# Products with the softmax's reciprocal and a clamp of weight words: VectorE or GpSimd

## The chip, the core and the metric

The kernel runs on one core of one Trainium2 chip. The metric is the device time of one execution in microseconds (us), median of the runs shown. Below, PE is TensorE (PEld its weight loads), DVE is VectorE, ACT is ScalarE, POOL is GpSimd, and SP is the engine whose queue issues all the transfers spoken of here. L299 means line 299 of the kernel.

## What is computed

Sliding-window attention with a linear bias, then a dense two-layer block with a squared rectifier, then a mixture of eight experts with a balanced gate. Cut to what the change touches:

```python
scores = scale * q @ k.T + bias                     # 4 batches, 8 heads, 576 tokens, head size 64
scores = np.where(mask, scores, -1e9)               # a window of 128 keys
attn = np.exp(scores - scores.max(-1))
attn = attn / (attn.sum(-1) + 1e-09)                # L296, L297, L299
x = attn @ v                                        # 2304 tokens x 512
h = np.maximum(x @ moe_w_in, 0.0)                   # 512 x 2048, float64 weights
x = (h * h) @ moe_w_out                             # 2048 x 512, float64 weights
...
```

The two weight matrices of the dense block come as float64. The kernel reads each number as two 32-bit words and builds a float32 pair from them.

## The kernel before

The work has two halves. The first, to about 600 us of the span, is attention and the dense block, and a scheduler orders each engine's instructions by its own estimates. The second half is the eight experts, in an order written out by hand (from L720 on, the manual schedule), and holds neither of the changed lines.

**Attention.** A unit is a pair of heads of one batch, either its first 384 tokens or its last 192 (`rest`); there are 32 units, with 80 tiles of up to 128 queries in all. `attention_scores` (L257) makes a tile's scores on PE (L282, name `sc`), adds the bias and takes the minimum on DVE (L285, `s` and `m`), takes the exponential and its sum on ACT (L292, `s` and `z`), and on DVE adds 1e-9 (L296), takes the reciprocal (L297) and multiplies (L299), for each of the two heads by itself. `attention_weights` (L302) turns the result on PE (L322, and L313 for the tail tile, name `pt`) and splits it into two float32r parts: ACT makes the high one, DVE the low one (L113, L114, `p`). `attention_values` multiplies with the values (L336, `xo`). PE does a later tile's scores before it turns an earlier tile (one or two tiles ahead, `plan`, L375).

**Dense block.** The tokens are cut into five chunks, the first of 384, and the hidden size into 16 slices `f`. For each chunk and slice, `gemm1` makes `h` (L118 to L120), ACT and DVE make the squared rectifier (L696, L698), ACT and POOL split it into `gh` and `gl` (L109, L110), and `moe1_tail` accumulates `acc` two slices later. In the first chunk alone, each slice's two weight tiles come from the float64 words: `fetch` (L458) loads 128x1024 words (name `u`, three buffers), `narrow` (L434) turns them into a float32 pair, and the pair is stored for the later chunks (L481). There are 32 calls of `narrow`. Each takes the magnitude on ACT (L440), scales the low words on ACT (L442), clamps the magnitude (L443), shifts (L444), joins (L447) and adds (L451) on DVE, and splits on ACT and DVE (L453, L454). The attention of the first 384 tokens comes ahead of the first chunk's products; the attention of the rest is spread between the products of the chunks.

The two lines of the change:

```python
            nc.vector.tensor_scalar_mul(s[:, j, :nk], s[:, j, :nk], z[:, j : j + 1])
...
        nc.vector.tensor_scalar(mag, mag, F64_SMALL, F64_LARGE, op0=ALU.max, op1=ALU.min)
```

Of the kernel before, what the change touches and what calls it, by code (L numbers as in the profile page):

```python
# [12 lines left out]
ALU = mybir.AluOpType  # L13
# [6 lines left out]
F64_SMALL = 2.0 ** -15  # L20
F64_LARGE = 122879.984375


def raw(ap):

    return ap.bitcast(F32)
# [3 lines left out]
def attention_moe_moe2(  # L30
# [12 lines left out]
    nc = tc.nc  # L43
# [118 lines left out]
    def at_ps(name, t, many=early):  # L162
        pool, tag = many[psn[0] % len(many)] if t["alone"] else (ps_at, "at")
        psn[0] += 1
        return pool.tile([P, 512], F32, name=name, tag=tag)
# [91 lines left out]
    def attention_scores(hp, t, i):  # L257

        tail = i == FULL

        kb0, qb0 = (2, 3) if t["rest"] else (0, 0)
        nk = min(S, (i + 1) * P) - max(0, i - 1) * P
        k0 = (max(0, i - 1) - kb0) * P
        c0 = 2 * P - nk if i == 0 else 0
        heads = 1 if tail else 2

        scs = [at_ps("sc", t) for j in range(heads)]
        s = ap.tile([P, 2, 2 * P], F32, name="s", tag="s", bufs=3)
        m = ap.tile([P, 2], F32, name="m", tag="m", bufs=3)
        z = ap.tile([P, 2], F32, name="z", tag="z", bufs=3)  # L270
        ops = []
        for j in range(heads):
            r = slice(0, P) if tail else slice(j * D, (j + 1) * D)
            if tail:
                qh, ql = [x.rearrange("p j c -> p (j c)") for x in t["qt"]]
            else:
                qh, ql = [t[n][r, (i - qb0) * P : (i - qb0 + 1) * P] for n in ("qh", "ql")]
            kh, kl = [t[n][r, k0 : k0 + nk] for n in ("kh", "kl")]
            ops.append(((qh, kh), (qh, kl), (ql, kh)))
        for x in range(3):  # L280
            for sc, (lhs, rhs) in zip(scs, [o[x] for o in ops]):
                nc.tensor.matmul(sc[:, :nk], lhsT=lhs, rhs=rhs, start=x == 0, stop=x == 2)  # L282
        for j, sc in enumerate(scs):
            bj = tbias[:, hp, :nk] if tail else bias[:, 2 * hp + j, c0 : c0 + nk]
            nc.vector.tensor_tensor_reduce(  # L285
                out=s[:, j, :nk], in0=sc[:, :nk], in1=bj, scale=1.0, scalar=3.0e38,
                op0=ALU.add, op1=ALU.min, accum_out=m[:, j : j + 1],
            )
        if tail:
            nc.gpsimd.memset(s[:, 0, nk:], 0.0)  # L290
        for j in range(heads):
            nc.scalar.activation(  # L292
                s[:, j, :nk], s[:, j, :nk], AF.Exp, bias=m[:, j : j + 1], scale=-1.0,
                accum_out=z[:, j : j + 1],
            )
        nc.vector.tensor_scalar_add(z[:, :heads], z[:, :heads], 1e-9)  # L296
        nc.vector.reciprocal(z[:, :heads], z[:, :heads])  # L297
        for j in range(heads):
            nc.vector.tensor_scalar_mul(s[:, j, :nk], s[:, j, :nk], z[:, j : j + 1])  # L299
        t[i] = s  # L300

    def attention_weights(t, i):  # L302
# [104 lines left out]
    def advance(n):  # L407
        for kind, m, i in steps[done[0] : n]:
            b, hp, rest = units[m]
            if kind == "q":  # L410
                if m == NPAIR:
                    tails_ready()
                attention_qk(m, ts[m])
                ts[m]["p"] = {}
            elif kind == "s":
                attention_scores(hp, ts[m], i)
                if i in (1, FULL):
                    attention_v(m, ts[m])
                    load(m + 2)
            else:  # L420
                attention_weights(ts[m], i)
                attention_values(b, hp, ts[m], i)
        done[0] = max(done[0], n)
# [10 lines left out]
    def narrow(src, hi, lo):  # L434

        low, high = src[:, :, 0], src[:, :, 1]
        t = [cv.tile([P, DM], U32, name=f"cv{i}", tag=f"cv{i}", bufs=2) for i in range(4)]

        mag = t[0].bitcast(F32)
        nc.scalar.activation(mag, high.bitcast(F32), AF.Abs)  # L440

        nc.scalar.activation(t[3], low, AF.Copy, scale=2.0 ** -29)  # L442
        nc.vector.tensor_scalar(mag, mag, F64_SMALL, F64_LARGE, op0=ALU.max, op1=ALU.min)  # L443
        nc.vector.tensor_scalar(  # L444
            t[1], t[0], 3, 0x3FFFFFF8, op0=ALU.logical_shift_left, op1=ALU.bitwise_and
        )
        nc.vector.scalar_tensor_tensor(  # L447
            t[2], high, 0xC0000000, t[1], op0=ALU.bitwise_and, op1=ALU.bitwise_or
        )

        nc.vector.tensor_add(t[1], t[2], t[3])  # L451
        w = t[1].bitcast(F32)
        nc.scalar.activation(hi, w, AF.Copy)  # L453
        nc.vector.tensor_sub(lo, w, raw(hi))  # L454
# [18 lines left out]
    def moe1_load(c, f):  # L473
        out = []
        for j, (nm, dr, nb) in enumerate((("a", d_in[f], 3), ("b", d_out[f], 4))):
            hl = mp.tile([P, 2, DM], F32R, name=nm, tag=nm, bufs=nb)
            if c == 0:
                i = 2 * f + j
                fetch(i + 2)
                narrow(words.pop(i), hl[:, 0], hl[:, 1])  # L480
                nc.sync.dma_start(dr, raw(hl))  # L481
            else:
                nc.sync.dma_start(raw(hl), dr)
            hl = [hl[:, 0], hl[:, 1]]
            out.append([x.rearrange("p (k f) -> p k f", k=NK) if nm == "a" else x for x in hl])
        return out
# [766 lines left out]
```

## Time and profile before

| what | us |
|---|---|
| median of 3 runs (2180.19 to 2181.93) | 2181.15 |
| the profiled execution | 2182.91 |
| its span, from the first instruction to the last | 2181.1 |
| busy: PE, DVE, ACT, POOL | 2101.9, 1513.8, 994.5, 1067.0 |
| PE idle in the span | 79.2 |

A busy time is a sum over the span; an engine that is idle while another sets the pace costs nothing. A stretch's limit shows in what PE, the busiest engine, waits for there. Spans on POOL are rough.

### The profile page before, as it was taken

The numbers are of one execution on the slowest core, as the hardware profiler recorded it, in microseconds if no ns is written. First come the engines' busy times: TensorE is split into PE (matmuls) and PEld (weight loads), VectorE is DVE, ScalarE is ACT, GpSimd is POOL, SyncE is SP. The second block draws the span as 40 slices with busy tenths as digits, with TensorE's granted clock in tenths as the row PEclk, the third lists the DMA queues.
The fourth block names the chain that finished last, engine by engine and source line by source line (L and its number), as shares of the span: only waits on it lengthen the run. The fifth ranks groups of instructions, "written<-read, shape, count | busy, mean of one in ns | idle before, by whom it ended". The sixth has DMA issues, their size and how long they took to land.

```text
span 2181.1 us, 32622 instructions
## 1 busy us (share of the span) xinstructions
PE 2101.9 (96%) x11360; PEld 1918.6 (88%) x11360; DVE 1513.8 (69%) x2667; ACT 994.5 (46%) x2050; POOL 1067.0 (49%) x709
## 2 busy tenths in 40 slices
PE   6889999999999899999999999999999999999998
PEld 4778777777888788888888899999999999999998
DVE  7998445443243888888888666667778567777666
ACT  6776445443334345444444444444444544444443
POOL 2212223123244777887878644445456445554442
PEclk9899999999999999999999999999999999999999
DMA  6676545545474877788788977777787877777773
GB/s 185 212 242 212 155 146 162 153 146 174 159 264 155 316 282 270 265 311 293 286 310 299 341 273 259 259 258 259 259 260 265 270 259 255 253 260 266 260 260 124
DMA packets 281730, 525.49 MB, mean 241 GB/s; under 512 B 85584, under 2 KB 129760, under 8 KB 277472
## 3 DMA queue, kind: packets, MB, share of 16 engines
q1 hardware_dynamic: 281568, 523.42, 71.2%
q8 instruction: 91, 1.49, 0.3%
q14 instruction: 71, 0.58, 0.1%
HBM read 379.60 MB, written 143.73 MB: 240 GB/s over the span
## 4 chain that ended last, share of the span: by engine, by line
PE 66%; DVE 21%; ACT 4%; issue 4%; DMA 3%; POOL 1%; SPq 1%; ACTq 0%; POOLq 0%; DVEq 0%
PE g L118 7%; PE y L119 7%; PE g L120 7%; PE g L119 7%; PE y L120 7%; PE y L118 7%; DVE o L904 4%; DVE rl L933 3%; PE h L118 3%; PE acc L118 3%; PE h L120 3%; PE h L119 3%; PE xo L336 3%; PE acc L120 3%; PE acc L119 2%
## 5 line engine op out<-in xcount | busy, mean ns | idle before, releaser
L1073 POOL TENSOR_TENSOR rb<-R,rb 128x768 fp32r<-128x768 f32 x95 | 212.4, 2237 | 334.4 <-ACT rb L1068 306.2
L1104 DVE TENSOR_TENSOR a<-y,a 128x384 f32<-128x384 f32 x434 | 239.8, 553 | 180.0 <-PE y L120 178.1
L1073 POOL TENSOR_TENSOR rt<-R,rt 128x768 fp32r<-128x768 f32 x125 | 238.7, 1922 | 146.7 <-issue 61.7
L110 POOL TENSOR_TENSOR gl<-r,gh 128x512 fp32r<-128x512 f32 (+1 forms) x80 | 98.9, 1237 | 354.5 <-ACT gh L109 339.7
L1068 ACT ACTIVATE rt<-R 128x768 fp32r<-128x768 f32 x128 | 107.7, 842 | 148.6 <-DVE R L1055 90.1
L110 POOL TENSOR_TENSOR w2a<-r,w2a 128x1024 fp32r<-128x1024 f32 x64 | 162.1, 2549 | 26.5 <-ACT w2a L109 26.4
L118 PE MATMUL g<-xt,w1o 128*128 128x384 f32 x512 | 172.7, 337 | 1.4 <-ACT u L809 0.6
L120 PE MATMUL g<-xt,w1o 128*128 128x384 f32 x512 | 172.2, 336 | 0.0
L118 PE MATMUL y<-rt,w2o 128*128 128x384 f32 x512 | 172.1, 336 | 0.1
L120 PE MATMUL y<-rt,w2o 128*128 128x384 f32 x512 | 172.1, 336 | 0.0
L119 PE MATMUL g<-xt,w1o 128*128 128x384 f32 x512 | 172.0, 336 | 0.0
L119 PE MATMUL y<-rt,w2o 128*128 128x384 f32 x512 | 171.8, 335 | 0.0
L119 PE MATMUL y<-w2a,rh 128*128 128x512 f32 x384 | 150.7, 392 | 2.3 <-POOL w2a L110 2.3
L118 PE MATMUL y<-w2a,rh 128*128 128x512 f32 x384 | 150.7, 393 | 0.0
L120 PE MATMUL y<-w2a,rl 128*128 128x512 f32 x384 | 150.1, 391 | 0.0
L698 DVE SCALAR_TENSOR_TENSOR r<-h,r 128x512 f32<-128x512 f32 (+1 forms) x80 | 50.9, 636 | 133.3 <-ACT r L696 133.3
L1050 DVE TENSOR_TENSOR R<-R,pb 128x768 f32<-128x768 f32 x128 | 137.8, 1077 | 5.2 <-ACT R L1163 3.0
L118 PE MATMUL y<-rb,w2o 128*128 128x384 f32 x384 | 129.9, 338 | 2.8 <-DVE a L1104 2.1
L119 PE MATMUL y<-rb,w2o 128*128 128x384 f32 x384 | 130.2, 339 | 2.4 <-POOL rb L1073 2.4
L120 PE MATMUL y<-rb,w2o 128*128 128x384 f32 x384 | 130.0, 339 | 0.0
L120 PE MATMUL g<-xb,w1o 128*128 128x384 f32 x384 | 129.0, 336 | 0.0
L118 PE MATMUL g<-xb,w1o 128*128 128x384 f32 x384 | 128.9, 336 | 0.0
(231 smaller groups left out, 6234.2 us busy)
## 6 DMA issues: line engine op xcount, KB each, us to landing
w1o<-d_w SPq DMA_DIRECT2D x448, 256.0 KB, 3.1
w2o<-d_w SPq DMA_DIRECT2D x224, 512.0 KB, 4.0
d_w<-w1a SPq DMA_DIRECT2D x32, 1792.0 KB, 12.1
d_w<-w2a SPq DMA_DIRECT2D x32, 1536.0 KB, 8.2
a<-d_in SPq DMA_DIRECT2D x64, 512.0 KB, 3.7
b<-d_out SPq DMA_DIRECT2D x64, 512.0 KB, 3.6
r<-in_moe_w_dram SPq DMA_DIRECT2D x64, 512.0 KB, 4.5
u<-in_moe_w_in_dram SPq DMA_DIRECT2D x16, 512.0 KB, 4.7
```

Of the source, the lines that this page charges most:

```text
L110: (eng or nc.gpsimd).tensor_sub(lo, src, raw(hi))
L118: nc.tensor.matmul(ps, lhsT=lh, rhs=rh, start=first, stop=False, **kw)
L119: nc.tensor.matmul(ps, lhsT=lh, rhs=rl, start=False, stop=False, **kw)
L120: nc.tensor.matmul(ps, lhsT=ll, rhs=rh, start=False, stop=last, **kw)
L336: nc.tensor.matmul(dst, lhsT=l, rhs=r, start=first and n == 0, stop=last and n == 5, skip_group_check=True)
L698: nc.vector.scalar_tensor_tensor(g[:, :n], ph[:, :n], 0.0, r[:, :n], op0=ALU.max, op1=ALU.mult)
L904: nc.vector.scalar_tensor_tensor(acc[0][:, i], y, pe[:, i, e : e + 1], acc[0][:, i], op0=ALU.mult, op1=ALU.add)
L933: nc.vector.scalar_tensor_tensor(rl, src, 0.0, raw(rh), op0=ALU.max, op1=ALU.subtract)
L1050: nc.vector.tensor_mul(r, r, pb[:, None, :].to_broadcast([P, 2, HALF]))
L1068: nc.scalar.activation(x[:, 0], R[m, f, h], AF.Copy)
L1073: eng.tensor_sub(x[:, 1], R[m, f, h], raw(x[:, 0]))
L1104: nc.vector.tensor_add(acc[dst][:, dt], ps[:, :HALF], acc[dst][:, dt])
```

## The change

Two operations go from DVE's queue to POOL's, with the same operands and tiles: the product of a head's exponentials with the reciprocal of their sum, and the clamp of the magnitude words.

```diff
@@ attention_scores
         nc.vector.reciprocal(z[:, :heads], z[:, :heads])
         for j in range(heads):
-            nc.vector.tensor_scalar_mul(s[:, j, :nk], s[:, j, :nk], z[:, j : j + 1])
+            nc.gpsimd.tensor_scalar_mul(s[:, j, :nk], s[:, j, :nk], z[:, j : j + 1])
@@ narrow
-        nc.vector.tensor_scalar(mag, mag, F64_SMALL, F64_LARGE, op0=ALU.max, op1=ALU.min)
+        nc.gpsimd.tensor_scalar(mag, mag, F64_SMALL, F64_LARGE, op0=ALU.max, op1=ALU.min)
```

Since the scheduler orders the first half, other instructions move too.

**POOL, the start of the program** (`bias` is the table of biases, `vsplit` the split values, `cv` a magnitude tile, `s` and `z` as above). Before:

```order
L152 AFFINE_SELECT bias<-bias 128x256 x2
L248 TENSOR_TENSOR vsplit_176<-vraw,vsplit_175 128x3x2x64
L248 TENSOR_TENSOR vsplit_170<-vraw,vsplit_169 128x3x2x64
L248 TENSOR_TENSOR vsplit_176<-vraw,vsplit_175 128x3x2x64
L248 TENSOR_TENSOR vsplit_170<-vraw,vsplit_169 128x2x2x64
```

After:

```order
L152 AFFINE_SELECT bias<-bias 128x256 x2
L443 TENSOR_SCALAR cv_291<-cv_291 128x512
L248 TENSOR_TENSOR vsplit_176<-vraw,vsplit_175 128x3x2x64
L443 TENSOR_SCALAR cv_307<-cv_307 128x512
L443 TENSOR_SCALAR cv_323<-cv_323 128x512
L299 TENSOR_SCALAR s<-s,z 128x128 x2
L443 TENSOR_SCALAR cv_339<-cv_339 128x512
L299 TENSOR_SCALAR s<-s,z 128x128 x2
L443 TENSOR_SCALAR cv_897<-cv_897 128x512
L299 TENSOR_SCALAR s<-s,z 128x256 x2
```

The first tile's two products now stand together behind the third clamp, and the second tile's behind the fourth.

**DVE, the same place** (`z` is the sum or its reciprocal). Before, the first reciprocal, with what follows it; after, the same:

```order
 L444 TENSOR_SCALAR cv_324<-cv_323 128x512
+L297 RECIPROCAL z<-z 128x2
+L296 TENSOR_SCALAR z<-z 128x2
+L447 SCALAR_TENSOR_TENSOR cv_325<-u,cv_324 128x512
 L454 TENSOR_TENSOR b<-cv_308,b 128x512
-L447 SCALAR_TENSOR_TENSOR cv_325<-u,cv_324 128x512
-L443 TENSOR_SCALAR cv_339<-cv_339 128x512
 L451 ISA cv_324<-cv_325,cv_326 128x1024
 L444 TENSOR_SCALAR cv_340<-cv_339 128x512
-L299 TENSOR_SCALAR s<-s,z 128x128
```

The reciprocal now comes behind the third shift (L444), and the product that stood behind the fourth is gone from this queue.

**POOL, the middle of the first chunk** (`gl` is the low part of the squared rectifier). After:

```order
L110 TENSOR_TENSOR gl<-r,gh 128x384
L290 MEMSET s 128x64
L443 TENSOR_SCALAR cv_1416<-cv_1416 128x512
L443 TENSOR_SCALAR cv_1521<-cv_1521 128x512
L299 TENSOR_SCALAR s<-s,z 128x256 x2
L443 TENSOR_SCALAR cv_1537<-cv_1537 128x512
L248 TENSOR_TENSOR vsplit_176<-vraw,vsplit_175 128x2x2x64
```

Before, this queue held only the `gl`, `vsplit` and memset rows here; now two products stand behind two clamps, each of which needs its words loaded.

## Rows read from the trace of the kernel before

**Rows 1.** Stretches: us, busy PE, PEld, DVE, ACT, POOL (count), clock, DMA share, GB/s.

```profile
0.00:20.00 20.00, 8.78 (x39) 6.22 (x39) 12.93 (x40) 13.34 (x34) 9.01 (x26) 1.00 0.72 188
20.00:200.00 180.00, 157.75 (x875) 132.22 (x876) 165.06 (x495) 127.80 (x351) 37.42 (x37) 0.93 0.70 217
200.00:600.00 400.00, 395.85 (x2072) 308.31 (x2070) 175.37 (x596) 173.84 (x492) 97.58 (x102) 1.00 0.52 158
600.00:2181.00 1581.00, 1539.47 (x8377) 1471.89 (x8377) 1160.48 (x1538) 679.51 (x1175) 923.00 (x545) 1.00 0.77 265
```

**Rows 2.** Waits of PE, 20 to 200 us: us in total, times, longest.

```profile
PE pt L322 <- DVE s L299: 10.6, 4, 6.0
PE pt L313 <- DVE m L285: 1.9, 1, 1.9
```

**Rows 3.** Timeline of PE: start, us, instruction, idle time before it and its releaser.

```profile
22.87 0.47 PE L322 MATMUL pt<-ident,s 128*128 128x128 f32 x1 [6.02 <-DVE s L299]
...
26.07 0.48 PE L322 MATMUL pt<-ident,s 128*128 128x128 f32 x1 [1.79 <-DVE s L299]
...
27.69 0.69 PE L322 MATMUL pt<-ident,s 128*128 128x128 f32 x2 [1.14 <-DVE s L299]
```

**Rows 4.** DVE's groups by shape, 0 to 200 us: count | busy us, mean ns.

```profile
L447 DVE SCALAR_TENSOR_TENSOR cv<-u,cv 128x512 uint32<-128x512 uint32 x32 | 24.7, 775 | 0.0
L451 DVE CUSTOM_DVE_ANT_0 cv<-cv,cv 128x1024 uint16<-128x1024 uint16 x32 | 22.3, 696 | 0.0
...
L443 DVE TENSOR_SCALAR cv<-cv 128x512 f32<-128x512 f32 x32 | 17.3, 552 | 0.5 <-ACT cv L440 0.4
...
L444 DVE TENSOR_SCALAR cv<-cv 128x512 uint32<-128x512 uint32 x32 | 14.6, 463 | 0.0
L299 DVE TENSOR_SCALAR s<-s,z 128x256 f32<-128x256 f32 x38 | 14.1, 412 | 0.0
L454 DVE TENSOR_TENSOR b<-cv,b 128x512 fp32r<-128x512 f32 x16 | 11.8, 736 | 1.9 <-ACT b L453 1.9
L454 DVE TENSOR_TENSOR a<-cv,a 128x512 fp32r<-128x512 f32 x16 | 11.1, 693 | 1.6 <-ACT a L453 1.6
...
L299 DVE TENSOR_SCALAR s<-s,z 128x128 f32<-128x128 f32 x16 | 4.1, 294 | 0.0
...
L299 DVE TENSOR_SCALAR s<-s,z 128x192 f32<-128x192 f32 x4 | 1.3, 314 | 0.0
```

**Rows 5.** POOL's groups by shape, 0 to 200 us: the one-input instructions.

```profile
L148 POOL TENSOR_SCALAR_AFFINE_SELECT bias<-bias 128x256 f32<-128x256 f32 x8 | 3.0, 399 | 0.0
...
masks.py:199 POOL TENSOR_SCALAR_AFFINE_SELECT ident<-ident 128x128 f32<-128x128 f32 x1 | 0.3, 292 | 0.0
```

**Rows 6.** POOL's groups by shape, 200 to 600 us: two-input instructions.

```profile
L110 POOL TENSOR_TENSOR gl<-r,gh 128x512 fp32r<-128x512 f32 x48 | 61.8, 1287 | 230.7 <-ACT gh L109 215.9 <-PE acc L120 11.4 <-DMA b<-d_out 3.4
...
L248 POOL TENSOR_TENSOR vsplit<-vraw,vsplit 128x256 fp32r<-128x256 f32 x11 | 8.0, 729 | 21.9 <-ACT vsplit L247 21.7
```

**Rows 7.** Single lines on DVE: minimum, median and maximum ns, first and last start.

```profile
L443 DVE TENSOR_SCALAR cv<-cv x32: 406/415/1310, 12.6 to 186.7; 128x512 f32<-128x512 f32 x32
L444 DVE TENSOR_SCALAR cv<-cv x32: 403/416/1071, 14.0 to 189.4; 128x512 uint32<-128x512 uint32 x32
L447 DVE SCALAR_TENSOR_TENSOR cv<-u,cv x32: 675/680/1507, 15.2 to 191.4; 128x512 uint32<-128x512 uint32 x32
```

**Rows 8.** Timeline of POOL: two instructions of the same line.

```profile
76.69 1.01 POOL L110 TENSOR_TENSOR gl<-r,gh 128x384 fp32r<-128x384 f32 x1 [6.54 <-ACT gh L109]
...
85.82 3.68 POOL L110 TENSOR_TENSOR gl<-r,gh 128x384 fp32r<-128x384 f32 x1 [8.03 <-ACT gh L109]
```

**Rows 9.** The chain that ended last, 0 to 210 us: start, us, what.

```profile
41.04 4.45 DMA u<-in_moe_w_in_dram
```

**Rows 10.** Waits of ACT, 20 to 200 us: us in total, times, longest.

```profile
ACT cv L440 <- DMA u<-in_moe_w_in_dram: 4.3, 4, 1.9
```

## The prediction

> **What bounds the kernel now.** I read the stretches first. From 600 us on PE is busy for 1539.47 of 1581 us and nothing that the change names runs; from 200 to 600 us PE is busy for 395.85 of 400 us while DVE has 175.37 and POOL 97.58 [rows 1]. There DVE is no bound, and relieving it can give at most the 4.15 us that PE idles. The stretch that can change is the first: from 20 to 200 us DVE is busy for 165.06 of 180 us (92%), PE for 157.75, ACT for 127.80 and POOL for 37.42 [rows 1]. PE idles 22.25 us there. The list of PE's waits in this stretch says for whom: 10.6 us for the products of L299 themselves, in four waits, then a row of single waits of 1 to 2 us for other DVE results, of which the first is 1.9 us [rows 2]. (A wait that began before 20 us is counted whole in that list.) Since DVE is 92% busy, these are waits for DVE's queue rather than for one instruction. The timeline shows the worst place: PE waits 6.02, 1.79 and 1.14 us for the first two tiles' products [rows 3].
>
> **The change, part by part.**
>
> *What leaves DVE.* Up to 200 us all 32 clamps (17.3 us) and 58 of the 144 products (14.1, 4.1 and 1.3 us), 36.8 us in all [rows 4]. DVE's 12.93 + 165.06 = 178.0 us up to 200 us become 141.2.
>
> *What POOL gets.* The trace has no such instruction on POOL. The near bound is its one-input instruction of the same shape: 399 ns for 256 columns, 292 for 128 [rows 5]; the difference, 107 ns for 128 columns, gives 345 ns for 192 and 613 for 512 as estimates. The far bound is its two-input instruction: 729 ns for 256 columns and 1287 for 512 [rows 6], hence 450 and 590 for 128 and 192. Near: 38 x 0.399 + 16 x 0.292 + 4 x 0.345 + 32 x 0.613 = 40.9 us. Far: 38 x 0.729 + 16 x 0.450 + 4 x 0.590 + 32 x 1.287 = 78.5 us. I take the near one, because both moved operations read one tile from SBUF and write one; the far end stays for the range. The Trainium skill (GPSIMD Engine Reference, section "Engine selection") says the same of one-input work, that it runs at about line rate, against half of VectorE's speed with two inputs; no run here shows it for this instruction.
>
> *What the two engines take from each other.* A clamp on DVE takes 415 ns in the median, but 1310 once, and L444 and L447 have such maxima too, 1071 and 1507 [rows 7]; a `gl` on POOL that takes 1.01 us elsewhere took 3.68 at 85.82 us [rows 8]. So they hold each other up. The means over the medians price it on DVE: (552 - 415) x 32 = 4.4 us, (463 - 416) x 32 = 1.5 and (775 - 680) x 32 = 3.0 [rows 4, 7], 8.9 us beside 9.01 + 37.42 = 46.4 us of POOL, or 0.19 us per us. For 40.9 us more on POOL that is 7.8 us. DVE's load to 200 us is then 141.2 + 7.8 = 149 us of 200 instead of 178: about 76% of the stretch from 20 us on instead of 92%.
>
> *The start (to 28 us).* The first tile's products now follow the reciprocal on an idle POOL, both heads at once, where PE got the two heads at 22.87 and 26.07 us and the second tile at 27.69 [rows 3]. That lets the first tiles go some 3 us earlier. But the words for the fifth tile of weights are on the chain, a 4.45 us load issued at 41.04 us [rows 9], behind a long row of attention loads on SP's queue, which waits for the store of the fourth tile; that store depends on DVE's L454 and moves by less. SP's queue is otherwise only reordered. I take -2 us.
>
> *The rest of the stretch.* Of the 22.25 us, (22.87 - 20) + 1.79 + 1.14 = 5.8 lie at the start; 16.4 remain, nearly all for DVE. The bounds are 0 and -16.4. With DVE's load down by a sixth, its queue still comes late where ACT makes it late (ACT is 71% busy, and waits for loads of words 4.3 us [rows 10]). I take a little under half: -7 us.
>
> *The handover.* A pair of products takes 2 x 0.4 us on POOL, where DVE's pair has 2 x 0.412 [rows 4, 5], but crosses engines, and may stand behind a clamp whose words have not come, or behind a `gl` of 1.29 us [rows 6]. The bounds are nothing, where PE has other tiles to do, and one `gl` for each of the four products that PE waited for today, 5 us. I take +1.
>
> *From 200 us on.* The other 86 products leave a DVE with room and join a POOL that is a quarter busy [rows 1]. The list of PE's waits there names no product, and PE has several us of other work between a tile's scores and its turning. I cost it at nothing. If that cover went, each late tile would cost PE up to one `gl`, 1.29 us; I allow +4.
>
> The sum is -2 - 7 + 1 = -8 us, against the profiled execution's 2182.91 us: 2174.9. That execution is 1.76 us above the median of the runs, so the forecast on their scale is **2173 us**.
>
> **The rivals.**
>
> *POOL's instructions are dearer, and the shared way to SBUF becomes the bound: slower.* The lines that were seen held up read or write SBUF on both engines. If only one of the two engines can do such work at a time, before the change that way is taken to 200 us by DVE's L443, L444, L447, L451, L454 and L299, 36.8 + 14.6 + 24.7 + 22.3 + 22.9 = 121.3 us [rows 4], and POOL's 46.4: 167.7 of 200. After it, DVE has 84.5 left, POOL 46.4 + 40.9: 171.8, still under 200. At the far price it is 84.5 + 46.4 + 78.5 = 209.4, over 200 by 9.4 us: 2190.5 us or more. The point from which it decides is 69 us of new work, 1.7 times the near price, or some 0.68 us for a 256-column product. The Trainium skill has this rule (SBUF — State Buffer, section "Who interferes with whom"): the shared port pair is an exclusive lock, held for a whole instruction, and the later comer blocks. The trace agrees with a blocked `gl` of 3.68 us. Against this rival speaks the 399 ns row.
>
> *Nothing gained: the next wait takes the place.* PE would wait for POOL's products, held behind clamps, or for the words that ACT waits for, as it now waits for DVE. For it speak rows 9 and 10, and that a held-up POOL instruction took 3.68 us. The terms cancel: 2177 to 2185 us. The Trainium skill (Perfetto Trace Analysis, section "Optimizing Scalar/DVE Operations") warns that moving work between these two engines might not help, for the shared port.
>
> *All of it gained.* PE's idle 16.4 us and 3 us at the start go: 2181.15 - 19.4 = 2162 us. PE's granted clock in the stretch, 0.93 between the levels of 2.4 and 1.2 GHz [rows 1], could rise with a busier PE and give some 2 us more; I count none of it in the sum.
>
> **How the numbers follow.** The forecast has a chance of 0.52, nothing gained 0.22, the shared way 0.16, all gained 0.10. A measurement of this kernel can tell about 0.2%, 4.4 us, from no change: faster means below 2176.8, slower above 2185.5. The forecast and the full gain count as faster, 0.62; the second rival as the same, 0.22; the first as slower, 0.16. For a range that holds the time 8 times in 10, I cut half of the full gain's and half of the first rival's: 2160 to 2189 us.
>
> **What would show it.** In the changed profile: POOL's L299 at 0.35 to 0.5 us for 256 columns and L443 near 0.6; DVE's share from 20 to 200 us down to about three quarters; the first turning of a tile at 21 to 22 us with both heads together; PE's waits for DVE in the stretch about halved, and PE's idle time from 200 us on unchanged. I am wrong if POOL's products take 0.7 us or more, if L444, L447 or L451 lengthen in the mean by over 0.25 us each, or if PE's list of waits now names POOL's L299 for 10 us or more.

## The result and the profile after

The change made the kernel **slower**: 2208.99 us (median of 5 runs, 2206.22 to 2220.29) against 2181.61 us for the kernel before in the same rounds (5 runs, 2180.19 to 2183.19). The ratio is 1.0133, 95% interval [1.0118, 1.0147]. The prediction said 2173 us, with a range to 2189. Repeated later, in other rounds, the changed kernel gave 1.0112 [1.0087, 1.0138].

The profiled execution of the changed kernel is the slowest of its five (2220.29 us, span 2218.1). Its stretches, with columns as in [rows 1], the second ending where PE begins the second chunk (its first product `h` with 512 columns, which began at 199.75 us before):

```profile
0.00:20.00 20.00, 8.42 (x39) 6.15 (x39) 10.31 (x33) 10.30 (x26) 12.60 (x28) 1.00 0.60 158
20.00:237.47 217.47, 182.55 (x884) 151.26 (x885) 150.83 (x417) 134.14 (x361) 151.22 (x127) 0.88 0.60 188
237.47:600.00 362.53, 360.19 (x1874) 279.50 (x1874) 140.80 (x475) 161.60 (x460) 155.92 (x174) 0.99 0.51 154
```

All of the loss lies in the first chunk: it ends 37.7 us later, and the span is 37.0 us longer. DVE is now busy for 150.83 of 217.47 us, 69%, where it was 92% [rows 1], but the stretch is longer: up to the second chunk DVE was busy 161.1 us, only 16.6 less than the 177.7 before. PE idles 34.9 us there, and the clock column reads 0.88, where it read 0.93; how far this column can be read is said at e15 below. What happened to the moved instructions shows in the views of single lines (minimum, median, maximum ns):

```profile
L299 POOL TENSOR_SCALAR s<-s,z x144: 596/923/2417, 23.1 to 629.8; 128x256 f32<-128x256 f32 x96, 128x128 f32<-128x128 f32 x32, 128x192 f32<-128x192 f32 x16
...
L443 POOL TENSOR_SCALAR cv<-cv x32: 1908/1921/2355, 13.6 to 214.4; 128x512 f32<-128x512 f32 x32
```

A product, mostly of 256 columns, takes 0.92 us on POOL in the median, against a mean of 0.41 on DVE [rows 4]; a clamp takes 1.92 us against 0.42 [rows 7]. The list of waits, 0 to 260 us (us in total, times, longest), shows who waits:

```profile
DVE cv L444 <- POOL cv L443: 27.2, 14, 3.6
POOL s L299 <- DVE z L297: 23.8, 15, 6.1
PEld pt L322 <- POOL s L299: 23.0, 12, 9.5
...
PE pt L322 <- POOL s L299: 13.7, 8, 9.2
```

DVE stands 27.2 us in front of the shift L444 for POOL's clamp, a wait that didn't exist, and everything else in DVE's queue stands behind it. PE waits 13.7 us for POOL's products, where it waited 10.6 us for DVE's [rows 2]. DVE's groups up to 237 us, with columns as in [rows 4], show the second price:

```profile
L447 DVE SCALAR_TENSOR_TENSOR cv<-u,cv 128x512 uint32<-128x512 uint32 x32 | 26.1, 818 | 0.4
L451 DVE CUSTOM_DVE_ANT_0 cv<-cv,cv 128x1024 uint16<-128x1024 uint16 x32 | 24.4, 764 | 0.3
L444 DVE TENSOR_SCALAR cv<-cv 128x512 uint32<-128x512 uint32 x32 | 19.2, 602 | 27.2 <-POOL cv L443 27.2
```

The same 32 instructions are longer in the mean than before: 818 against 775, 764 against 696, 602 against 463 ns [rows 4]. The start of the program shows both prices together. POOL's timeline (start, us, instruction, idle time before it and its releaser):

```profile
20.22 2.28 POOL L443 TENSOR_SCALAR cv<-cv 128x512 f32<-128x512 f32 x1 [1.84 <-ACT cv L440]
23.14 2.33 POOL L299 TENSOR_SCALAR s<-s,z 128x128 f32<-128x128 f32 x2 [0.63 <-DVE z L296]
25.44 1.92 POOL L443 TENSOR_SCALAR cv<-cv 128x512 f32<-128x512 f32 x1
27.99 1.90 POOL L299 TENSOR_SCALAR s<-s,z 128x128 f32<-128x128 f32 x2 [0.63 <-DVE z L297]
```

And PE's:

```profile
24.75 0.47 PE L322 MATMUL pt<-ident,s 128*128 128x128 f32 x1 [9.24 <-POOL s L299]
...
33.45 0.69 PE L322 MATMUL pt<-ident,s 128*128 128x128 f32 x2 [1.18 <-POOL s L299]
```

The first tile turns at 24.75 us instead of 22.87 [rows 3], and tiles and clamps alternate on POOL at some 2 us each.

### The profile page after: what moved, and what is told of

The parts are those of the page before. It is cut to its first block, busy times and chain, and to the rows that moved or that the text cites. A ratio compares the mean times of both kernels' runs of the same rounds, so it can differ in the third digit from the quotient of the medians.

```text
span 2218.1 us, 32804 instructions
## 1 busy us (share of the span) xinstructions
PE 2129.7 (96%) x11360; PEld 1941.8 (88%) x11360; DVE 1468.0 (66%) x2491; ACT 997.7 (45%) x2050; POOL 1255.5 (57%) x885
## 3 DMA queue, kind: packets, MB, share of 16 engines
q8 instruction: 91, 1.49, 0.3%
## 4 chain that ended last, share of the span: by engine, by line
PE 68%; DVE 18%; ACT 4%; POOL 3%; issue 3%; DMA 2%; SPq 0%; ACTq 0%; POOLq 0%; DVEq 0%
PE y L119 7%; PE y L120 7%; PE y L118 7%; PE g L118 7%; PE g L120 7%; PE g L119 7%; DVE o L904 4%; PE xo L336 3%; DVE rl L933 3%; PE h L118 3%; PE acc L118 3%; PE acc L120 3%; PE h L119 3%; PE h L120 3%; PE acc L119 3%
## 5 line engine op out<-in xcount | busy, mean ns | idle before, releaser
L299 POOL TENSOR_SCALAR s<-s,z 128x256 f32<-128x256 f32 (+1 forms) x144 | 131.6, 924 | 103.3 <-DVE z L297 82.8
L110 POOL TENSOR_TENSOR w2a<-r,w2a 128x1024 fp32r<-128x1024 f32 x64 | 161.1, 2533 | 27.9 <-ACT w2a L109 27.9
L118 PE MATMUL y<-rb,w2o 128*128 128x384 f32 x384 | 129.8, 338 | 2.8 <-DVE a L1104 2.1
L119 PE MATMUL y<-rb,w2o 128*128 128x384 f32 x384 | 130.0, 338 | 2.3 <-POOL rb L1073 2.3
L118 PE MATMUL acc<-gh,b 128*128 128x512 f32 (+1 forms) x320 | 131.3, 410 | 0.0
L118 PE MATMUL h<-xh,a 128*128 128x512 f32 (+1 forms) x320 | 128.3, 401 | 2.3 <-DVE r L698 2.2
```

Source lines behind the costliest of these rows:

```text
L110: (eng or nc.gpsimd).tensor_sub(lo, src, raw(hi))
L118: nc.tensor.matmul(ps, lhsT=lh, rhs=rh, start=first, stop=False, **kw)
L119: nc.tensor.matmul(ps, lhsT=lh, rhs=rl, start=False, stop=False, **kw)
L299: nc.gpsimd.tensor_scalar_mul(s[:, j, :nk], s[:, j, :nk], z[:, j : j + 1])
```

## The experiments

The theories, as the expectations name them. **A**: POOL's price and turn-taking; the loss is time in which DVE and PE wait for POOL's long instructions. **B**: the two engines hold each other up at SBUF, so that POOL's work costs DVE time even if nobody waits for its results. **C**: the scheduler's new order alone. A fourth, **D**, came with the profile: PE's pauses lower the clock that it is granted. All kernels below are the kernel before with the edit shown. "Us" is the ratio's distance from 1 times 2182 us.

| run | on POOL | ratio to before [95%] | us |
|---|---|---|---|
| e1_products | the products | 1.0029 [1.0011, 1.0046] | +6.3 |
| e2_clamp | the clamps | 1.0057 [1.0038, 1.0075] | +12.4 |
| e15_both_again | both (the change) | 1.0112 [1.0087, 1.0138] | +24.4 |
| e12_shadow_products | extra products, nobody waits | 1.0038 [1.0023, 1.0054] | +8.3 |
| e8_shadow_free | extra clamps, nobody waits | 1.0058 [1.0042, 1.0074] | +12.7 |
| e14_shadow_both | both extra loads, nobody waits | 1.0049 [1.0029, 1.0069] | +10.7 |
| e3_shadow | extra clamps that hold a buffer | 1.0109 [1.0067, 1.0150] | +23.8 |
| e7_one_op | the clamps, one operation | 1.0018 [1.0005, 1.0030] | +3.9 |
| e13_both_one_op | both, clamps with one operation | 1.0088 [1.0063, 1.0112] | +19.2 |
| e5_two_input | the products as two-input ones | 1.0040 [1.0021, 1.0058] | +8.7 |
| e4_low | the split's low part (L454) | 1.0071 [1.0052, 1.0089] | +15.5 |
| e6_late | the later tiles' products | 0.9998 [0.9982, 1.0013] | -0.4 |
| e9_swap | nothing | 0.9997 [0.9985, 1.0008] | -0.7 |
| e10_drop_add | nothing; L296 left out | 0.9996 [0.9978, 1.0014] | -0.9 |
| e11_act_one | nothing; half the products on ACT | 0.9992 [0.9977, 1.0007] | -1.7 |

**One part at a time.**

```diff
e1_products
-            nc.vector.tensor_scalar_mul(s[:, j, :nk], s[:, j, :nk], z[:, j : j + 1])
+            nc.gpsimd.tensor_scalar_mul(s[:, j, :nk], s[:, j, :nk], z[:, j : j + 1])
e2_clamp
-        nc.vector.tensor_scalar(mag, mag, F64_SMALL, F64_LARGE, op0=ALU.max, op1=ALU.min)
+        nc.gpsimd.tensor_scalar(mag, mag, F64_SMALL, F64_LARGE, op0=ALU.max, op1=ALU.min)
```

> The 144 products on GpSimd, the clamps back on VectorE. Theory A (price and turn-taking): a GpSimd product takes 0.9 us for 256 columns where VectorE took 0.35, and TensorE waits for the turning behind it; the products cost about half of the loss, +10 to +15 us over the kernel before, and GpSimd's products keep their 0.9 us. Theory B (the two engines block each other at SBUF): the loss goes with GpSimd's added busy time up to the end of the first chunk, some 50 of 113 us, so about +12 us, and VectorE's L444, L447 and L451 lengthen in the mean by over 0.1 us each. Theory C (the scheduler's new order alone): under +5 us, with GpSimd's products not named in TensorE's waits.

> The 32 clamps on GpSimd, the products back on VectorE. Theory A: 1.92 us for a clamp, and VectorE's L444 waits for it 15 to 27 us in all; since VectorE is relieved of 17 us and each weight tile is wanted two slices later, the loss is +5 to +15 us. Theory B: about 63 of 113 us of added GpSimd time, so about +15 us, with L444, L447 and L451 longer by over 0.1 us each. Theory C: under +5 us.

Each part loses by itself, the clamps some twice as much, and the products less than either theory A or B gave for them. The waits of DVE for the clamps alone are far smaller than with both (e2's profiled execution is the fastest of its six):

```profile
DVE cv L444 <- POOL cv L443: 8.6, 6, 3.0
```

8.6 us here, 27.2 with the products on the same queue: there a clamp that is ready stands behind products and a product behind clamps.

**POOL busy, nobody waiting.** e8 and e12 leave DVE all of its work and give POOL a second load of the same shapes, which reads other tiles and writes a scratch tile that nobody reads; e14 has both. In e12 and e14 the reciprocals get eight buffers, so that POOL holds none up; no run has these buffers without the load. (e3 was the first try: its copy reads the magnitude itself and so keeps its buffer from ACT, which then waited 15.3 us for POOL. It mixes A and B.)

```diff
e8_shadow_free, behind L454
+        beside = cv.tile([P, DM], F32, name="beside", tag="beside", bufs=1)
+        nc.gpsimd.tensor_scalar(beside, raw(hi), F64_SMALL, F64_LARGE, op0=ALU.max, op1=ALU.min)
e12_shadow_products, behind L299 (bj: the tile's bias)
+            beside = ap.tile([P, 2 * P], F32, name="beside", tag="beside", bufs=1)
...
+            nc.gpsimd.tensor_scalar_mul(beside[:, :nk], bj, z[:, j : j + 1])
e3_shadow, behind L443
+        nc.gpsimd.tensor_scalar(beside, mag, F64_SMALL, F64_LARGE, op0=ALU.max, op1=ALU.min)
```

> The kernel before, and in addition each clamp is done once more on GpSimd into a tile that nobody reads. VectorE is not relieved and nobody waits for GpSimd's copy, but GpSimd is busy for 61 us more up to the end of the first chunk. Theory A: within +4 us of the kernel before (what the two engines take from each other is small). Theory B: at least as dear as the clamps moved alone, +15 us or more. Theory C: whatever the order gives, within 5 us either way.

> The kernel before, and in addition 32 clamps of 128x512 on GpSimd that read the high part of each weight tile, which is not given free before a product two slices later, and write a tile nobody reads. GpSimd is busy for some 61 us more in the first chunk, and nobody waits for these instructions' results or buffers. Theory A (waiting for GpSimd's results and buffers): within 4 us of the kernel before. Theory B (blocking at SBUF): +8 us or more, and VectorE busy for 10 us more up to the end of the first chunk.

> The kernel before with an extra GpSimd product of the same shapes beside each of DVE's 144 products: it reads the bias tile and the reciprocal and writes a scratch tile that nobody reads (the reciprocals get more buffers, so that nothing waits for it). GpSimd gets the load of the products of L299, some 40 x 1.1 us more up to 200 us, DVE keeps its own, nobody waits for GpSimd. The run with the products alone on GpSimd was 6.4 us slower, with DVE relieved of 19.5 us. Theory A (price and turn-taking: the loss is waiting for the products): 0 to +3 us. Theory B (the engines hold each other up at SBUF): at 0.19 us of DVE per us of GpSimd some 8 us more on DVE, and a loss of 6 to 12 us, as the extra clamps that nobody waits for cost 12 us. Theory C (the scheduler's order alone): any sign, within 5 us.

> The kernel before with both extra loads on GpSimd at once, the 32 clamps that read the weights' high words and the 144 products that read the bias, into scratch tiles: GpSimd gets the changed kernel's work, DVE keeps all of its own, and nothing waits for GpSimd. Alone they cost 12 and 8 us. Theory B (hindrance at SBUF is all of the loss): some 20 to 27 us, and more where the two overlap; the changed kernel, whose DVE is relieved of 37 us, would then lose less than this one. Theory A (the waits for GpSimd are the loss): under 10 us. If B and A share it: 15 to 20 us here, against 27 with the waits.

POOL's work costs time even if nobody waits for it: 12.7 and 8.3 us alone, 10.7 with both, so B is shown to be a part of it, though e14's 10.7 is less than the 15 to 20 expected if A and B share the loss. That the two together cost no more than one I can't explain; the intervals allow some of it ([6.3, 15.1] against a sum of 21 with some 5 either way). The stretches of e14 up to its second chunk:

```profile
0.00:20.00 20.00, 8.78 (x39) 6.22 (x39) 12.71 (x38) 13.01 (x33) 11.23 (x27) 1.00 0.72 190
20.00:211.19 191.19, 165.03 (x873) 138.58 (x874) 180.81 (x498) 128.60 (x351) 163.64 (x125) 0.91 0.66 204
```

DVE is busy 12.71 + 180.81 = 193.5 us with the work that took it 177.7 up to 199.75 us before: 15.8 us more, for 128.7 us more on POOL (174.9 against 46.2), or 0.12 us per us. In e8 it is 11.7 us for 73.6 (0.16), in e12 8.0 for 62.0 (0.13). e14's groups on DVE in the same stretch (the shifted lines are L443, L444, L447, L451, L454 of before):

```profile
L454 DVE CUSTOM_DVE_ANT_0 cv<-cv,cv 128x1024 uint16<-128x1024 uint16 x32 | 24.2, 756 | 0.0
L450 DVE SCALAR_TENSOR_TENSOR cv<-u,cv 128x512 uint32<-128x512 uint32 x32 | 23.2, 731 | 0.0
...
L299 DVE TENSOR_SCALAR s<-s,z 128x256 f32<-128x256 f32 x38 | 17.7, 505 | 0.0
L447 DVE TENSOR_SCALAR cv<-cv 128x512 uint32<-128x512 uint32 x32 | 17.4, 550 | 0.0
L446 DVE TENSOR_SCALAR cv<-cv 128x512 f32<-128x512 f32 x32 | 17.2, 553 | 0.8 <-ACT cv L443 0.8
...
L457 DVE TENSOR_TENSOR b<-cv,b 128x512 fp32r<-128x512 f32 x16 | 14.2, 889 | 1.7 <-ACT b L456 1.7
L457 DVE TENSOR_TENSOR a<-cv,a 128x512 fp32r<-128x512 f32 x16 | 12.0, 749 | 0.1
```

These groups sum to 125.9 us, and POOL's 174.9 make 300.8 us in 211.2. At least 89.6 us of these recorded spans lie side by side. A span can hold time in which the instruction is held up, as the 3.68 us of [rows 8] may, so each form is also counted at its shortest duration in this stretch: DVE's groups then take 102 us and POOL's 147, together 249 us in 211.2. One at a time doesn't hold them, by some 38 us. Hence the engines hinder each other, but the way is not given to one of them alone.

**How long POOL's instruction is.**

```diff
e7_one_op
-        nc.vector.tensor_scalar(mag, mag, F64_SMALL, F64_LARGE, op0=ALU.max, op1=ALU.min)
+        nc.gpsimd.tensor_scalar_max(mag, mag, F64_SMALL)
e13_both_one_op: e7_one_op with e1_products
e5_two_input
-            nc.vector.tensor_scalar_mul(s[:, j, :nk], s[:, j, :nk], z[:, j : j + 1])
+            nc.gpsimd.tensor_mul(s[:, j, :nk], s[:, j, :nk], z[:, j : j + 1].to_broadcast([P, nk]))
```

> The clamp alone on GpSimd, with one of its two operations (the maximum; the minimum is left out). With both it took 1.92 us for 512 columns, and the kernel 12.5 us more. If each operation costs a pass of its own, it takes 1.0 to 1.3 us, DVE's waits for it go from 8.6 to about 4 us, and the loss falls to 5 to 8 us (theories A and B alike, A by the waits, B by GpSimd's 22 us less). If a pass has one price whatever it computes, 1.9 us and +12 us.

> Both moved as in the change, but GpSimd's clamp with one operation (the minimum is left out), 1.49 us instead of 1.92, so that GpSimd has 14 us less to do up to the end of the first chunk. The clamp alone cost 12.5 us with two operations and 3.9 with one, the products alone 6.4. If GpSimd's length of work is what counts (A by the waits, B by the time held), the loss falls from 27 us to 10 to 14. If it stays above 20 us, the length of the clamp is not the cause of what the two cost together.

> The changed kernel once more, on the same chip and in the same rounds as the two others, for comparison with them and for its granted clock over more executions: it was 0.981 to 0.989 in five, against 0.986 to 0.993 in the kernel before. Expected: +25 to +29 us. If pauses of PE lower the granted clock (D), the mean clock stays some 0.003 below that of before, worth 6 to 8 us of the 27, while the runs with one part alone showed the clock of before within 0.001.

> Products on GpSimd as in the run with the products alone, but written as a product of two tiles (the reciprocal repeated along the row), the form in which GpSimd took 0.73 us for 256 columns of the values' split. Clamps on VectorE. Theory A (GpSimd's price): if a product takes 0.73 to 0.8 us instead of 0.92 to 1.15, the time falls below that of the run with the products alone, to +1 to +5 us over the kernel before. Theory B (blocking at SBUF): a second input read from SBUF holds VectorE up more, as the low parts did when they went to GpSimd; +8 us or more, with VectorE's L444 and L451 longer by over 0.15 us in the mean than in the kernel before.

The clamp's line in e7:

```profile
L443 POOL TENSOR_SCALAR cv<-cv x32: 1479/1492/2449, 13.9 to 184.4; 128x512 f32<-128x512 f32 x32
```

The second operation costs 0.43 us of the 1.92, between the two guesses. With 14 us less on POOL the clamp alone loses 3.9 us instead of 12.4, less than the 5 to 8 expected, though with both parts the loss falls only from 24.4 to 19.2, short of what was expected. In e13 DVE still waits for the clamps 19.7 us and PE for products 13.7. In e5 the line of the products reads:

```profile
L299 POOL TENSOR_TENSOR s<-s,z x144: 394/614/1147, 20.2 to 600.5; 128x256 f32<-128x256 f32 x96, 128x128 f32<-128x128 f32 x32, 128x192 f32<-128x192 f32 x16
```

The same product, asked for as a two-input instruction, takes 614 instead of 923 ns in the median. It gained nothing (+8.7 against +6.3, intervals overlapping), but it is no clean test of the length: up to the second chunk POOL was busy 81.9 us in e5 and 107.5 in e1, but DVE 170.7 and 165.2, so part of what POOL saved was paid on DVE.

e15 is the more typical execution of the changed kernel. Its stretches:

```profile
0.00:20.00 20.00, 8.41 (x39) 6.14 (x39) 10.14 (x33) 10.25 (x26) 12.60 (x28) 1.00 0.59 154
20.00:232.09 212.09, 174.47 (x885) 143.79 (x885) 150.12 (x417) 134.33 (x361) 150.66 (x127) 0.93 0.62 193
```

The first chunk ends 32.3 us later than before, and the span is 27.1 us longer. PE idles 91.3 us of the span, 12.0 more than before, and its busy time grows by 15.1 us for the same 11360 matmuls. That is no added work, and it bears on D. The clock column reads 0.93 in the first chunk, as before, and its mean over the five executions is 0.988, over the 13 of before in those rounds 0.989. But the column counts time without a clock record as full clock, and the records begin only at 74.5 us in e15 and at 33.2 us in the kernel before. Which of the two levels (1.2 and 2.4 GHz) PE had until then shows in the multiplications with the values (L336). The first line is the kernel before from 46.9 to 57.0 us, with 0.50 recorded; the second the same from 33.2 to 46.8 us, with 1.00 recorded; the third e15 from 20 to 74.4 us, without a record:

```profile
L336 PE MATMUL xo<-p,vsplit 128*128 128x256 f32 x7 | 2.2, 460 | 0.0
L336 PE MATMUL xo<-p,vsplit 128*128 128x256 f32 x21 | 4.3, 316 | 0.2
L336 PE MATMUL xo<-p,vsplit 128*128 128x256 f32 x42 | 12.7, 456 | 1.1 <-DVE p L114 0.6 <-DMA qraw<-in_q_dram 0.5
```

So in e15 PE ran at the lower level up to 74.5 us, where in the kernel before it rose at 33.2. In the first chunk 289 of e15's 924 matmuls began at the lower level, against 139 of 912. Over the chunk the means of this form nearly agree at each level (456 and 455 ns at the lower, 309 and 298 at the higher), and so do those of the other frequent forms. So the 15.1 us are, as nearly as the trace tells, the clock's, and D is not refuted: more than half of the 27.1 us is PE at its lower level. What that is worth by itself is open. The first record comes at 64 to 75 us in the changed kernel, e1, e5, e7, e13 and e15, and at 33 to 40 us in the kernel before and the other ten; yet e7 loses 3.9 us, and in e5 PE's busy time grows by 14.7 us while its idle time falls by 9.5. Before its rise PE was busy, in the kernel before, for 6.9 of the 13.1 us from 20 us on; in e15 for 5.4 of 16 us from 20 us on and for 34.8 of the next 38.4. Why it stayed low that long, no run here tells.

**What relief of DVE is worth, and other controls.** e6 moves only products behind the first chunk, e11 gives half of them to ACT, e10 leaves out the addition of 1e-9, e9 exchanges two lines of text, and e4 gives POOL another step of `narrow` in the place of the clamp.

```diff
e6_late
-            nc.vector.tensor_scalar_mul(s[:, j, :nk], s[:, j, :nk], z[:, j : j + 1])
+            eng = nc.vector if t["early"] else nc.gpsimd
+            eng.tensor_scalar_mul(s[:, j, :nk], s[:, j, :nk], z[:, j : j + 1])
e11_act_one, for j = 1 alone
+                nc.scalar.activation(s[:, j, :nk], s[:, j, :nk], AF.Copy, scale=z[:, j : j + 1])
e10_drop_add
-        nc.vector.tensor_scalar_add(z[:, :heads], z[:, :heads], 1e-9)
e9_swap
-        nc.scalar.activation(t[3], low, AF.Copy, scale=2.0 ** -29)
         nc.vector.tensor_scalar(mag, mag, F64_SMALL, F64_LARGE, op0=ALU.max, op1=ALU.min)
+        nc.scalar.activation(t[3], low, AF.Copy, scale=2.0 ** -29)
e4_low
-        nc.vector.tensor_sub(lo, w, raw(hi))
+        nc.gpsimd.tensor_sub(lo, w, raw(hi))
```

> Only the products of the later units go to GpSimd (batch 1's last rows and batches 2 and 3, some 84 products, which come after the first chunk); clamps and the earlier products stay on VectorE. TensorE is the bound there. Both theories: within 3 us of the kernel before. If these late products cost over 5 us, the loss is not confined to the first chunk.

> The second head's product of each tile goes from DVE to ACT as a scaled copy, GpSimd gets nothing. DVE loses half of the products, some 10 us up to 200 us; ACT, 71% busy there, gets 29 of them at 0.4 to 0.6 us, some 14 us. Theory A and the prediction's reasoning (a relieved DVE lets PE wait less): -3 to -6 us, if ACT has the room. Theory B: the same sign, since ACT doesn't share GpSimd's way to SBUF: -3 to -6 us. If ACT's queue then comes later than DVE's did (it waits for loads of words, and the product stands behind them): 0 to +8 us, with PE's waits naming ACT's L299.

> The kernel before without L296, which adds 1e-9 to the softmax's sum; a sum that holds exp(0) = 1 does not change by it in float32. It takes 28 small instructions of 0.17 us off VectorE up to 200 us, and off each tile's chain. If VectorE's queue bounds the first chunk, as the prediction had it, 2 to 6 us faster than the kernel before; if not, within 2 us.

> The kernel before with two independent lines of the program's text exchanged, ACT's scaled copy (L442) and DVE's clamp (L443): the same instructions on the same engines, only the scheduler's priorities of the two differ. Theories A and B: no difference, within 3 us. Theory C (the new order of the scheduled program alone makes such differences): some 5 us or more in either direction.

> Clamps and products on VectorE; instead the low part of each weight tile (L454, 32 subtractions with two inputs of 128x512) goes to GpSimd, 1.29 us each there against 0.69 on VectorE. Nobody waits for it before a store and a product two slices later. Theory A: VectorE is relieved of 22 us and no chain gets longer: 3 to 8 us faster than the kernel before. Theory B: GpSimd's 41 us more block VectorE: no gain or up to 8 us slower.

The late products cost nothing, and the exchanged lines move the time by -0.7 us [-3.3, +1.7]: and e6, e10 and e11, which move instructions too, also lie within 2 us of the kernel before. Nothing here shows that a new order alone could cost 24 us, so C is unlikely as the cause. e11 is the answer to the question that the prediction didn't ask. On ACT it has the group

```profile
L300 ACT ACTIVATE s<-s,z 128x256 f32<-128x256 f32 (+1 forms) x28 | 13.2, 471 | 0.1
```

with DVE's first chunk 5.8 us lighter (172.0 busy), and it gains 1.7 us [-5.0, +1.5], which is not told from nothing. PE's longest wait for a product is 5.4 us, in front of the half that stayed on DVE, against 6.0 before [rows 2]:

```profile
PE pt L325 <- DVE s L302: 9.3, 3, 5.4
```

e4 missed by the sign. It took 22.9 us from DVE [rows 4], and DVE was busy 182.0 us up to its second chunk, more than before:

```profile
0.00:20.00 20.00, 8.78 (x39) 6.21 (x39) 12.66 (x35) 12.26 (x31) 10.44 (x27) 1.00 0.68 184
20.00:210.50 190.50, 160.34 (x882) 136.19 (x882) 169.39 (x475) 131.31 (x353) 75.92 (x68) 0.92 0.68 211
```

For 40.2 us more on POOL, what is left on DVE grew by 27.2 us, 0.68 us per us, four to five times the price of the one-input loads that nobody waits for.

**What follows.** Of the 24.4 us, 10.7 [6.3, 15.1] come with POOL's work alone (e14). The other 14, within some 7, come only where its results are needed; this is a difference of two runs, and since no run has the waits without the load, that waiting is the cause of it is argued, not shown. On PE, e15's longer span is 15.1 us of matmuls at the lower clock and 12.0 of idle time; e14's is 8.0 and 3.9. How much of the clock's part follows from PE's waits is open. The wait that grows most when the parts are put together is DVE's for the clamp (8.6 alone; 25.4 in e15). No kernel tried beats the kernel before by more than the measurement can tell.

## Why the prediction was wrong

**The step that failed first: *What POOL gets*.** It took the near price, "because both moved operations read one tile from SBUF and write one": 0.399 us for 256 columns and 0.613 for 512, 40.9 us in all [rows 5]. The first chunk of e15 has these groups:

```profile
L443 POOL TENSOR_SCALAR cv<-cv 128x512 f32<-128x512 f32 x32 | 63.7, 1994 | 10.7 <-ACT cv L440 10.7
L299 POOL TENSOR_SCALAR s<-s,z 128x256 f32<-128x256 f32 x40 | 42.9, 1083 | 16.4 <-DVE z L297 10.8 <-ACT b L453 3.7 <-ACT s L292 1.1
...
L299 POOL TENSOR_SCALAR s<-s,z 128x128 f32<-128x128 f32 x16 | 14.4, 908 | 13.0 <-DVE m L285 5.7 <-DVE z L297 3.9 <-ACT b L453 2.7
```

That is 121.0 us, and 124.6 with the tiles of 192 columns: three times the near price and 1.6 times the far end of 78.5. (The two sums, worked out again, come to 40.8 and 78.4, which changes nothing.) The far end was no bound, since one row of another operation (of two inputs) doesn't bound a form that the trace doesn't hold. The Trainium skill (GPSIMD Engine Reference, section "Engine selection") puts one-input work on GpSimd at about line rate; these rows don't agree, for the one-input product took 923 ns in the median on POOL, where the two-input one took 614 and DVE's 412 in the mean of 256 columns [rows 4].

***What the two engines take from each other*** was right in its price, 0.19 us of DVE per us of POOL: e15's DVE is busy 160.3 us up to its second chunk. Without the moved work (17.3 us of clamps and some 20 of products) 140 were left; 20 us more for 117 on POOL is 0.17. Only the number of us was wrong, 20 instead of 7.8. DVE's share fell to 69 or 71%, below the 76% forecast, but over a longer stretch: its 160.3 us are less than the 177.7 before and more than the forecast 149.

***The handover*** was the second step that failed. It gave +1 us and at most 5, for the products that PE waits for. It left the clamp's own handover out, which the next instruction on DVE needs at once: 25.4 us of waiting on DVE in front of L444 in e15, with all of DVE's queue behind. Its sentence "a pair of products takes 2 x 0.4 us on POOL" is the first step's mistake carried on: the first pair took 2.33 us.

***The start* and *the rest of the stretch*** forecast -2 and -7 us from a relieved DVE. The first tile came 1.9 us later instead of 3 earlier. The reading under it, that a queue busy to 92% makes PE's waits, is not borne out: e11 relieved DVE without touching POOL and gained 1.7 us [-5.0, +1.5], e10 0.9 [-4.8, +3.1]. So the 16.4 us of PE's idle time were no measure of what a lighter DVE gives. e11's relief is small, though, and a larger one without POOL was not tried.

***The clock*** stood at nothing in the sum ("I count none of it in the sum"), and only as a gain. It was a third step that failed: e15's matmuls took 15.1 us more, of which the lower level is, as nearly as the trace tells, the whole. The 1.00 and 0.93 of [rows 1] also hide that the kernel before ran at the lower level up to 33.2 us.

***From 200 us on*** was right: e6 has the products there on POOL and no difference.

**The rivals.** The first ended on the right side, and its deciding point was passed: 124.6 us of new work against 69, 0.92 us for a product against 0.68. Its mechanism holds only in part. With one engine at a time, e14 would have had 102 + 147 = 249 us of work for the shared way even at the shortest durations, which the chunk's 211 us can't hold. The Trainium skill's rule of an exclusive lock (SBUF — State Buffer, section "Who interferes with whom") therefore does not set the time of this mix as a whole, though the lengthened lines and e4 agree that there is a hindrance. Of the prediction's three signs of error two came: products over 0.7 us, and PE waiting over 10 us for POOL's L299. The third, lines longer by over 0.25 us, did not: the largest was 0.14, L444. The second rival, that the next wait takes the place, came in kind (DVE's wait for the clamp) but not in its size, which ended at 2185 us.

## What to carry to other kernels

Price an instruction on GpSimd by a row of the same operation with the same kind of operands, or leave the bound open above: here the form, not the count of inputs, set 0.40, 0.61 or 0.92 us for a tile of mostly 256 columns. When work leaves a busy engine for a slower one, list who needs each result next, and what is queued behind that reader; a chain DVE to GpSimd to DVE stops DVE's whole queue. Before counting on relief, ask what one us less on the busy engine has been shown to buy; here it bought next to nothing. Before reading a clock column, see from where on it has records, and compare matmuls of one form in both kernels.

## What the runs showed of the hardware

GpSimd's product with a scalar per partition (mostly of 256 columns) takes 923 ns in the median, and the same product with the reciprocal broadcast as a second input 614. A clamp of 512 columns takes 1.92 us with two operations and 1.49 with one. What work on GpSimd takes from VectorE beside it depends on the instruction: 0.12 to 0.16 us per us for one-input work that nobody waits for (e8, e12, e14), some 0.27 for the moved clamps (e2: 177.1 us on DVE against 177.7 - 17.3, for 62.7 on POOL), 0.68 for the two-input subtraction (e4). A multiplication of 256 columns (L336) takes 455 to 460 ns at TensorE's lower clock level and 298 to 316 at the higher; the lower one held from the start to 33 us in the kernel before and to 74 us in e15.
